# Row maxima and the second norm's later transposes moved from TensorE to VectorE, with a new instruction order

## The chip, the core and the metric

The kernel runs on one core of one Trainium2 chip. The metric is the device time of one execution in microseconds. Fp32 products are made of fp32r pieces: an operand is split into a rounded part and a remainder, and three matmuls (rounded by rounded, and the two cross terms) give the product.

## The reference, cut to what matters

`D` is 512, the sequence 2048 rows in `N` = 4 segments of `L` = 512, with 32 heads of 16.

```python
def _A_ref(x, wq, wk, wv, wo, beta):          # x is the normed input
    # q, k, v: (x @ w) in heads and segments
    mask = (ar[:, None] < ar[None, :]) * (-1e9)
    for s in range(N):
        logits = einsum("bhqd,bhkd->bhqk", qs, ks) * scale + mask
        p = softmax(logits)
        a_dot = einsum("bhqk,bhkd->bhqd", p, vs)
        a_mem = (phi(qs) @ M) / (phi(qs) . z + 1e-6)
        outs.append(g * a_mem + (1.0 - g) * a_dot)
        M = M + phi(ks)^T vs;  z = z + sum phi(ks)
    return o @ wo
def _B_ref(x, w_gate, w_up, w_down):
    return (gelu(x @ w_gate) * (x @ w_up)) @ w_down      # inner width 1376
h  = x + _A_ref(_layernorm(x), ...)
h2 = h + _B_ref(_layernorm(h), ...)
```

## The kernel before, in words

**Attention.** The work is cut into 16 units, one for a chunk of 8 heads and a segment, each in two halves of 4 heads; a half is called `Q` below and there are 32 of them. `qkv` projects a unit (TensorE line L874 for q and k, L913 for v), ScalarE and VectorE split the results, and DMAs lay them out by heads in tiles `stq` and `stk`. `pass_a(Q)` makes all scores of the half once (TensorE L1109), adds the causal mask and takes the negated row maximum on VectorE (L1119, each time followed by a read-out of the accumulator into `nm`). GpSimd splits the maxima in two parts, a rounded one (L1133) and its remainder (L1134), in a 128x32 tile `mm` (the variable `m2`). Two TensorE transposes (L1140), one for 64 partitions each, turn it into two PSUM banks, and two ScalarE copies (L1144) bring both into the 32x128 tile `mx`, of which there is one. A DMA (L1147) writes `mx` into rows of `stq` that were left free for it, so that the next pass's score matmul subtracts the maximum by itself. `pass_b(Q)` makes the scores again, transposed (TensorE L1167), takes the exponential (ScalarE L1173), cuts the diagonal blocks (GpSimd L1181), and multiplies by v (TensorE L1195, in column tiles of 32). Sums, division and the memory part `a_mem` follow through DRAM tiles.

**Feed-forward part.** `wo_seg(s)` multiplies by `wo` and adds x; the sum goes to `h_dram`. `ln2` norms 512 rows and transposes them. The product with the gate and up weights is made for two blocks of 512 rows at once by a scheme with seven products in the place of eight (`ffn`, TensorE L1456), and `down` multiplies by the down weights (TensorE L1520, sum on VectorE L1528). This runs for `p` = 0 and `p` = 1, each 1024 rows. The two calls of `ln2` for `p` = 0 transpose in row tiles of TensorE (`by_side`). The two calls for `p` = 1 load rows again from `h_dram`, norm them on ScalarE (`off`), and transpose them by 16 TensorE matmuls of 128x128 each (L833); of each result ScalarE and VectorE make split blocks.

**Order.** Every helper (`pe`, `act`, `dve`, `pool`, `dma`) only records an operation. `S.run(ORDER)` issues the operations in the sequence of the table `ORDER`, a list of their numbers written out by hand or by a program beforehand; each engine works through its own queue in that sequence. Buffers of a pool are handed out in the same sequence: 35 tiles `row`, 18 tiles `slot`, 8 PSUM banks.

Of the kernel before, what the change touches and what calls it, by code (L numbers as in the profile page):

```python
# [15 lines left out]
P = 128  # L16
# [40 lines left out]
    4, 6, 13, 8, 10, 12, 5, 61, 9, 7, 11, 14, 15, 16, 17, 75, 30, 18, 19, 76, 0, 28, 72, 73, 787, 791, 32, 74,  # L57
    65, 20, 84, 24, 21, 77, 22, 78, 81, 26, 86, 792, 23, 793, 79, 71, 29, 31, 27, 25, 35, 788, 1, 33, 80, 82,
    60, 64, 789, 87, 88, 66, 133, 794, 83, 795, 134, 89, 600, 990, 130, 90, 109, 36, 34, 37, 91, 92, 94, 93, 62,
    85, 2, 98, 38, 135, 99, 39, 994, 995, 996, 796, 110, 797, 104, 103, 43, 131, 111, 798, 112, 67, 799, 42,  # L60
    105, 114, 152, 63, 147, 800, 801, 155, 156, 132, 153, 150, 97, 116, 784, 154, 1386, 96, 142, 143, 113, 144,
    115, 219, 220, 70, 100, 41, 221, 40, 151, 136, 146, 148, 149, 44, 145, 597, 222, 106, 137, 59, 107, 45, 139,
    138, 46, 140, 95, 997, 802, 51, 101, 223, 790, 2085, 49, 141, 157, 52, 47, 158, 102, 224, 803, 53, 56, 48,
    50, 804, 108, 58, 179, 181, 182, 225, 159, 160, 127, 226, 161, 785, 183, 54, 805, 2276, 117, 119, 227, 162,
    57, 163, 118, 180, 404, 129, 228, 55, 165, 229, 164, 205, 174, 176, 178, 230, 405, 233, 806, 208, 177, 209,
    122, 786, 236, 991, 237, 206, 175, 195, 198, 199, 406, 598, 196, 169, 170, 407, 173, 232, 242, 241, 207,
    408, 200, 203, 171, 197, 231, 243, 128, 201, 172, 166, 167, 204, 409, 168, 202, 190, 191, 193, 211, 212,
    234, 184, 807, 410, 214, 411, 808, 185, 186, 244, 235, 3, 194, 192, 187, 1571, 213, 238, 809, 412, 810, 599,
    215, 413, 188, 189, 263, 123, 239, 415, 210, 266, 267, 998, 265, 216, 258, 601, 264, 240, 260, 68, 372, 811,
    262, 414, 261, 259, 416, 812, 289, 217, 246, 245, 124, 591, 373, 292, 293, 294, 290, 291, 1574, 297, 298,  # L70
    295, 296, 252, 374, 813, 814, 815, 253, 999, 254, 279, 375, 255, 376, 1000, 256, 257, 284, 280, 281, 282,
    283, 287, 288, 594, 268, 1001, 218, 1383, 992, 125, 285, 286, 270, 269, 272, 377, 300, 271, 301, 303, 378,
    332, 379, 327, 335, 336, 333, 334, 328, 380, 330, 592, 273, 274, 381, 275, 276, 277, 382, 69, 602, 299, 278,
    393, 304, 331, 394, 302, 305, 386, 383, 329, 384, 385, 400, 763, 306, 319, 764, 320, 321, 390, 348, 395,
    322, 396, 397, 765, 326, 325, 351, 352, 353, 398, 387, 766, 120, 323, 356, 767, 349, 388, 354, 399, 392,
    993, 781, 324, 316, 350, 391, 121, 247, 248, 307, 249, 364, 365, 569, 318, 317, 768, 343, 357, 367, 346,
    443, 344, 447, 769, 358, 445, 770, 359, 403, 126, 361, 444, 438, 446, 355, 366, 442, 441, 347, 771, 337,
    338, 339, 360, 389, 341, 552, 340, 772, 1002, 402, 362, 440, 432, 423, 775, 773, 368, 439, 433, 424, 345,
    363, 593, 434, 369, 342, 448, 774, 370, 474, 1003, 401, 308, 477, 449, 478, 553, 2088, 782, 783, 310, 452,
    417, 554, 475, 371, 419, 450, 418, 459, 476, 555, 451, 435, 462, 469, 460, 463, 311, 472, 556, 461, 436,  # L80
    464, 557, 473, 437, 507, 309, 453, 425, 454, 470, 467, 465, 471, 595, 573, 468, 508, 558, 819, 466, 480,
    483, 747, 559, 510, 481, 512, 560, 576, 574, 511, 312, 313, 509, 513, 455, 479, 516, 250, 1004, 514, 575,
    579, 596, 482, 484, 485, 456, 1190, 561, 577, 562, 578, 251, 457, 458, 563, 502, 1005, 1191, 504, 503, 515,
    564, 1192, 1193, 568, 486, 567, 1006, 565, 506, 499, 581, 523, 505, 1194, 566, 816, 580, 314, 487, 524, 538,
    1007, 1195, 541, 542, 501, 496, 525, 500, 498, 497, 1196, 528, 539, 540, 526, 527, 529, 530, 1197, 531, 532,
    533, 517, 623, 1198, 426, 626, 536, 625, 537, 627, 624, 733, 1008, 534, 535, 488, 315, 544, 734, 751, 1200,
    518, 1199, 1380, 612, 613, 571, 1202, 1201, 614, 519, 547, 735, 520, 628, 490, 817, 521, 522, 489, 631, 630,
    736, 632, 737, 615, 629, 543, 617, 548, 616, 491, 818, 545, 570, 603, 583, 649, 604, 605, 1009, 546, 738,
    650, 652, 639, 640, 642, 641, 739, 654, 618, 619, 622, 621, 657, 658, 620, 653, 655, 549, 550, 644, 647,
    740, 645, 660, 663, 661, 427, 633, 634, 741, 428, 1010, 1011, 656, 648, 572, 584, 635, 742, 743, 492, 636,  # L90
    1012, 637, 429, 430, 431, 1013, 754, 582, 752, 651, 420, 755, 638, 753, 643, 646, 744, 659, 662, 664, 745,
    756, 665, 759, 666, 955, 757, 719, 1014, 585, 720, 758, 421, 1015, 1016, 1017, 1018, 683, 586, 684, 746,
# [1530 lines left out]
```

## Time and profile before

| what | value |
|---|---|
| median of 3 runs | 762.25 us (759.47 to 766.43) |
| profiled execution | 760.04 us |
| its span, first to last instruction | 758.3 us |
| granted TensorE clock | 0.999 |
| instructions | 18030 |
| DMA packets | 70346, 103.66 MB |

The span is what the profile's rows divide up; the profiled execution's own time is 1.7 us longer. Attention fills the span up to about 400 us, the feed-forward part the rest. PE is TensorE's matmul, PEld its weight load, DVE VectorE, ACT ScalarE, POOL GpSimd and SP the engine that issues nearly all DMAs.

### The profile page before, as it was taken

How to read it: one execution, taken by the hardware profiler on the slowest of the kernel's cores; microseconds unless marked ns; L12 is line 12 of the kernel's file. 1: busy time of each engine (PE TensorE's matmuls, PEld its weight loads, DVE VectorE, ACT ScalarE, POOL GpSimd, SP SyncE). 2: the span in 40 equal slices, each digit the busy share in tenths (PEclk: the TensorE clock that was granted, in tenths of full speed). 3: DMA queues.
4: the chain of work that ended last, by engine and by line, in shares of the span. 5: the costliest groups of instructions: out<-in, count | busy, mean ns of one | idle time of the engine just before them, and what ended most of it. 6: DMA issues, size and time to landing. Idle time of an engine off the chain costs nothing.

```text
span 758.3 us, 18030 instructions
## 1 busy us (share of the span) xinstructions
PE 740.1 (98%) x6222; PEld 588.0 (78%) x6222; DVE 579.6 (76%) x1786; ACT 504.5 (67%) x1060; POOL 481.8 (64%) x748
## 2 busy tenths in 40 slices
PE   7899999999999999999999999899999999999997
PEld 5787877768778777776768788788888878888886
DVE  6798789988888898899977455865679645666566
ACT  5887987888776878867685455566675455544640
POOL 6454534644544656677985678786789577869740
PEclk9999999999999999999999999999999999999999
DMA  7666466764666675776658553322123260000002
GB/s 266 174 189 162 119 166 177 193 160 125 173 174 175 174 211 172 197 211 185 193 190 271 185 198 114 119 70 70 56 67 122 70 222 0 1 1 0 1 1 111
DMA packets 70346, 103.66 MB, mean 137 GB/s; under 512 B 12800, under 2 KB 23600, under 8 KB 70256
## 3 DMA queue, kind: packets, MB, share of 16 engines
q1 hardware_dynamic: 69952, 102.13, 46.4%
q8 instruction: 49, 0.80, 0.4%
q10 hardware_dynamic: 304, 0.39, 0.2%
q14 instruction: 41, 0.34, 0.1%
HBM read 54.92 MB, written 21.43 MB: 101 GB/s over the span
## 4 chain that ended last, share of the span: by engine, by line
PE 53%; DVE 3%; POOL 3%; ACT 1%; issue 1%; DMA 0%; POOLq 0%
PE bank L1456 26%; PE bank L1520 15%; PE bank L1275 3%; PE bank L1268 2%; PE bank L1195 2%; PE bank L1167 1%; PE bank L1109 1%; PE bank L874 1%; DVE bank L1119 1%; POOL row L1181 1%; POOL row L1433 1%; POOL slot L1426 1%; PE bank L833 0%; DVE row L1528 0%; DMA r_dram<-z 0%
## 5 line engine op out<-in xcount | busy, mean ns | idle before, releaser
L1173 ACT ACTIVATE row<-bank 128x512 f32<-128x512 f32 x306 | 164.1, 605 | 30.0 <-PE bank L1167 27.6
L1181 POOL TENSOR_SCALAR_AFFINE_SELECT row<-row 128x256 f32<-128x256 f32 (+1 forms) x306 | 106.1, 368 | 104.6 <-ACT row L1173 102.0
L1119 DVE CUSTOM_DVE_ANT_0 aside<-bank,amask 128x128 f32<-128x128 f32 (+2 forms) x384 | 141.2, 419 | 17.0 <-PE bank L1109 9.1
L874 PE MATMUL bank<-slot,slot 64*128 64x512 f32 x720 | 113.7, 404 | 0.7 <-DVE nm L1119 0.6
L1456 PE MATMUL bank<-slot,slot 128*128 128x512 f32 (+1 forms) x381 | 102.3, 391 | 0.0
L1119 DVE CUSTOM_DVE_ANT_0 bank<-bank,amask 128x512 f32<-128x512 f32 x128 | 86.2, 711 | 6.5 <-PE bank L1109 5.7
L1109 PE MATMUL bank<-stk,stq 64*128 64x128 f32 (+3 forms) x512 | 85.5, 333 | 1.9 <-issue 0.7
L1167 PE MATMUL bank<-stq,stk 64*128 64x512 f32 (+3 forms) x512 | 84.4, 337 | 1.2 <-DVE nm L1119 0.7
L1456 PEld LDWEIGHTS bank<-slot,slot 128*128 128x128 f32 (+1 forms) x381 | 70.2, 186 | 16.5 <-DVE bank L1309 0.4
L1528 DVE TENSOR_TENSOR row<-row,bank 128x512 f32<-128x512 f32 x84 | 55.6, 679 | 35.8 <-PE bank L1520 35.6
L874 PEld LDWEIGHTS bank<-slot,slot 64*128 64x128 f32 x720 | 74.9, 185 | 6.7 <-DVE nm L1119 1.2
L1195 PE MATMUL bank<-row,vaug 128*32 128x512 f32 (+3 forms) x982 | 77.2, 435 | 1.0 <-DVE nm L1119 0.2
L1426 POOL TENSOR_TENSOR slot<-row,slot 128x512 fp32r<-128x512 f32 (+3 forms) x52 | 59.5, 1148 | 26.9 <-ACT slot L1424 26.8
L1109 PEld LDWEIGHTS bank<-stk,stq 64*128 64x128 f32 x512 | 59.7, 184 | 14.9 <-DVE nm L1119 4.6
L1167 PEld LDWEIGHTS bank<-stq,stk 64*128 64x128 f32 x512 | 56.9, 185 | 15.2 <-DVE nm L1119 4.0
L1520 PE MATMUL bank<-slot,slot 128*128 128x512 f32 (+2 forms) x231 | 60.4, 387 | 0.0
L1195 PEld LDWEIGHTS bank<-row,vaug 128*32 128x32 f32 x982 | 30.5, 109 | 35.9 <-issue 30.6
L913 PE MATMUL bank<-slot,slot 64*128 64x256 f32 x672 | 54.4, 284 | 0.1
L913 PEld LDWEIGHTS bank<-slot,slot 64*128 64x128 f32 x672 | 49.7, 186 | 1.3 <-DVE slot L971 0.8
L668 POOL TENSOR_TENSOR slot<-row,slot 128x512 fp32r<-128x512 f32 (+1 forms) x33 | 42.7, 1297 | 12.5 <-ACT slot L663 12.3
L1520 PEld LDWEIGHTS bank<-slot,slot 128*128 128x128 f32 (+1 forms) x231 | 43.0, 188 | 9.1
L1119 DVE DVE_READ_ACCUMULATOR2_ANT nm<- 128x1 f32 x512 | 49.8, 97 | 0.1
(263 smaller groups left out, 1650.1 us busy)
## 6 DMA issues: line engine op xcount, KB each, us to landing
stq<-slot SPq DMA_DIRECT2D x96, 128.0 KB
stk<-slot SPq DMA_DIRECT2D x94, 128.0 KB
pv_dram<-row SPq DMA_DIRECT2D x32, 256.0 KB
row<-x SPq DMA_DIRECT2D x29, 256.0 KB
row<-r_dram SPq DMA_DIRECT2D x26, 256.0 KB
row<-h_dram SPq DMA_DIRECT2D x21, 256.0 KB
row<-wg SPq DMA_DIRECT2D x18, 256.0 KB
row<-wd SPq DMA_DIRECT2D x18, 256.0 KB
```

The costliest lines, as they stand in the source:

```text
L874: return nc.tensor.matmul(pm[i].t, w[i].t[rows_of(r), wi, dc * P:(dc + 1) * P], XT[s][dc].t[rows_of(r), xi, :], start=(dc, wi, xi, ph) == ...
L913: return nc.tensor.matmul(pms[n].t[:, 256 * t:256 * t + 256], XT[s][dc].t[rows_of(r), xi, t0:t0 + P], whl[wi].t[rows_of(r), dc // 2, 256 * ...
L1109: nc.tensor.matmul(sa.t[:, c0:c0 + w], sq.t[own, p, i * P:(i + 1) * P], sk.t[own, p, 0:w], start=True, stop=True, tile_position=(64 * a, 0 ...
L1119: nc.vector.tensor_tensor_reduce(out=(sa.t[:, c0:c0 + w] if i > 2 else aside[:, turns[0]:turns[0] + w]), in0=sa.t[:, c0:c0 + w], in1=amask ...
L1167: nc.tensor.matmul(sc.t[:, c0:c0 + D - q0], sk.t[own, p, q0:q0 + P], sq.t[own, p, q0:D], start=True, stop=True, tile_position=(64 * a, 0), ...
L1173: act(w, prio, lambda sc=sc, e=e: nc.scalar.activation(e.t[:, :w], sc.t[:, :w], AF.Exp), [sc, vtab], [e])
L1181: nc.gpsimd.affine_select(v, v, pattern=pat + [[1, P]], compare_op=OP.is_ge, fill=0.0, base=0, channel_multiplier=-1)
L1195: nc.tensor.matmul(pv.t[32 * n:32 * n + 32, kb * P:D], va.t[:, 136 * kb + 17 * j:136 * kb + 17 * j + 32], e.t[:, lo:lo + D - kb * P], star ...
L1426: pool(0.14 + 2.13e-3 * (hi - lo), prio, lambda: nc.gpsimd.tensor_tensor(v.t[:, 1, :hi - lo], r.t[:, lo:hi], v.t[:, 0, :hi - lo].bitcast(F ...
L1456: nc.tensor.matmul(dst.t[:w], v.t[:, wi, c0 + j * w:c0 + (j + 1) * w], b[bk][j].t[:, xi, :], start=first and j == 0 and n == 0, stop=j == ...
L1520: nc.tensor.matmul(pm.t[:, cs], HH[p, f, s].t[:w, hi, t * P:(t + 1) * P], v.t[:w, wi, cs], start=f == fl[0] and n == 0, stop=f == fl[-1] a ...
L1528: dve(W_, prio, lambda a=a, pm=pm, cs=cs, to=to: nc.vector.tensor_tensor(to.t[:, cs], a.t[:, cs], pm.t[:, cs], op=OP.add), [pm, a], [to])
```

## The change

The maxima: the two TensorE transposes and the two ScalarE copies of a half are replaced by four VectorE transposes of 32x32, from `m2` straight into `mx`. The two PSUM banks are no longer taken.

The second norm, for `p` = 1: VectorE transposes each normed 128x512 tile in 32x32 blocks into another `row` tile. Four DMAs for each tile store it, 32 partitions each, to a DRAM tile `t_dram` so that the blocks land in transposed places (runs of 32 elements, 128 bytes). Four DMAs for each norm load 128x512 tiles back, and ScalarE copies each into a PSUM bank, where the split goes on as before.

The table `ORDER` is new as a whole. Lines of the changed kernel that have a counterpart stand 10 to 14 lines further down.

```diff
@@ ORDER
-    4, 6, 13, 8, 10, 12, 5, 61, 9, 7, 11, 14, 15, 16, 17, 75, 30, 18, 19, 76, 0, 28, 72, 73, 787, 791, 32, 74,
+    6, 10, 8, 12, 5, 9, 7, 11, 84, 0, 1, 75, 14, 15, 16, 18, 72, 73, 4, 771, 2, 970, 13, 81, 17, 19, 28, 74,
...
+    t_dram = dram.tile([2, D, D], F32, name="t_dram")
...
@@ layer_norm(..., swap=None)
+        vt = Val()
+        for t in range(4) if swap is not None else []:
+            q = Val(PN)
+            dve(D, prio, lambda t=t, q=q: nc.vector.transpose(q.t, rows[t].t), [rows[t]], [q])
+            for a in range(4):
+                dma(prio, lambda t=t, q=q, a=a: nc.sync.dma_start(bass.AP(
+                    tensor=swap.tensor, offset=swap.offset + t * P + 32 * a,
+                    ap=[[D, 32], [32 * D, 16], [1, 32]]), q.t[32 * a:32 * a + 32]), [q], [vt], kb=480, dur=0.5,
+                    chain=True)
+        for dc in range(ND) if swap is not None else []:
+            dma(prio, lambda dc=dc: nc.sync.dma_start(rows[dc].t, swap[dc * P:(dc + 1) * P]), [vt], [rows[dc]])
         for dc in [] if by_side else range(ND):
             pt = Val(PD)
-
-            def tr(dc=dc, pt=pt):
-                for t in range(4):
-                    nc.tensor.transpose(pt.t[:, t * P:(t + 1) * P],
-                                        rows[t].t[:, dc * P:(dc + 1) * P], ident)
-            pe(4 * TR, prio, tr, [*rows, vident], [pt], acq=acq[dc] if acq else [dst[dc]])
+            if swap is not None:
+                act(D, prio, lambda dc=dc, pt=pt: nc.scalar.activation(pt.t, rows[dc].t, AF.Copy), [rows[dc]], [pt],
+                    acq=acq[dc] if acq else [dst[dc]])
+            else:
+                def tr(dc=dc, pt=pt):
...
@@ pass_a
-        m2, pts, mx = Val(PMM), (Val(PA), Val(PA)), Val(PMX)
+        m2, mx = Val(PMM), Val(PMX)
...
         def turn():
-            for i, pt in enumerate(pts):
-                own = rows_of(i)
-                nc.tensor.transpose(pt.t[0:32, 0:64], m2.t[own].bitcast(F32).rearrange("p a r i -> p (a r i)"),
-                                    ident[own, own], tile_position=(64 * i, 0))
-        pe(rr(64), prio, turn, [m2, vident], pts, acq=[mx], head=0.12, mode="r")
-        for i, pt in enumerate(pts):
-            act(64, prio, lambda i=i, pt=pt: nc.scalar.activation(
-                mx.t[:, 64 * i:64 * i + 64], pt.t[0:32, 0:64], AF.Copy), [pt], [mx], src=0.13, chain=True)
+            for i in range(4):
+                own = slice(32 * i, 32 * i + 32)
+                nc.vector.transpose(mx.t[:, own], m2.t[own].bitcast(F32).rearrange("p a r i -> p (a r i)"))
+        dve(330, prio, turn, [m2], [mx])
...
@@ the second norm of p = 1
-                    ln2(B[1], rows, s, prio, True, PD)
+                    ln2(B[1], rows, s, prio, True, PD, swap=t_dram[s])
```

Where the turn stands. Before, on TensorE, in the sixth half: scores of the next half, the two transposes, then a projection.

```order
L1109 MATMUL bank_70<-stk_92,stq_97 128x512
L1109 MATMUL bank_67<-stk_92,stq_97 128x512
L1140 MATMUL bank_71<-ident,mm_155 32x64
L1140 MATMUL bank_66<-ident,mm_155 32x64
L874 MATMUL bank_72<-slot_75,slot_86 128x512
L874 MATMUL bank_65<-slot_75,slot_85 128x512
```

Now, on VectorE, in the eleventh half, at the place with the fewest instructions between the last maximum of the half (written to `nm_152`) and its turn (which reads `mm_154`, made from it by GpSimd). ISA is the masked maximum and, with 128x1, the read-out that follows it.

```order
L1133 ISA bank_68,nm_152<-bank_68,amask 128x512
L1133 ISA nm_152 128x1
L1133 ISA bank_65,nm_152<-bank_65,amask 128x512
L1133 ISA nm_152 128x1
L545 COPY tock<-bank_68 128x1
L1154 STREAM_TRANSPOSE mx_156<-mm_154 32x32 x4
L1133 ISA aside,nm_153<-bank_65,amask 128x384
L1133 ISA nm_153 128x1
L1133 ISA aside,nm_153<-bank_65,amask 128x128
```

The turn has left TensorE's queue and stands in VectorE's, ahead of maxima of the next half.

The second norm. Before, on TensorE, in the feed-forward part: groups of four transposes between products of `ffn`.

```order
L1456 MATMUL bank_66<-slot_82,stq_100 128x512 x3
L833 MATMUL bank_67<-ident,row_122 128x128
L833 MATMUL bank_67<-ident,row_121 128x128
L833 MATMUL bank_67<-ident,row_128 128x128
L833 MATMUL bank_67<-ident,row_103 128x128
L1456 MATMUL bank_71<-slot_81,slot_86 128x512 x3
```

Now, on SP: the stores of the turned tiles (L833 of the changed kernel) and the first loads (L838) stand between loads of feed-forward weights (`wg`) and of rows of `h_dram`.

```order
L833 DMA t_dram<-row_124 32x16x32 x2
L833 DMA t_dram<-row_107 32x16x32
L833 DMA t_dram<-row_124 32x16x32
L1560 DMA row_126<-h_dram 128x512
L833 DMA t_dram<-row_107 32x16x32 x3
L838 DMA row_112<-t_dram 128x512
L833 DMA t_dram<-row_132 32x16x32
L838 DMA row_127<-t_dram 128x512
L1429 DMA row_102<-wg 128x512
```

On ScalarE the copies into PSUM (L842) stand between splits of weights and steps of the gate (L1434, L1494, L1473).

```order
L1494 ACTIVATE slot_80<-row_132 128x512
L842 ACTIVATE bank_70<-row_112 128x512
L1494 ACTIVATE stk_94<-row_134 128x512
L663 ACTIVATE slot_84<-row_115 128x512
L1434 ACTIVATE slot_74<-vaug_142 128x256
L856 ACTIVATE slot_87<-bank_70 128x512
```

TensorE has no instruction of the second half's norm any more; DMAs on SP's queue and copies on ScalarE's take their place.

More of the change, by code (lines that the diff above doesn't have):

```diff
@@ L686, in split_wv, with layer_norm @@
                 chain=True)
-    def layer_norm(prio, rows, dst, off=False, keep=None, acq=None, done=(), behind=(), scratch=None, by_side=False):
+    def layer_norm(prio, rows, dst, off=False, keep=None, acq=None, done=(), behind=(), scratch=None, by_side=False, swap=None):
         bn, mv = Val(PBN), Val(PMV)
@@ L1298, in blocks, with ln2 @@
         return {k: [Val(PBL), Val(PBL)] for k in ("11", "21", "t1", "22", "t3", "t2", "t4")}
-    def ln2(b, rows, i, prio, off, scratch=None, by_side=False):
+    def ln2(b, rows, i, prio, off, scratch=None, by_side=False, swap=None):
         ys = [Val(PC), Val(PC)] if i else []
@@ L1345, in ln2 @@
         if i == 0:
-            layer_norm(prio, rows, [*b["11"], *b["21"]], off=off, scratch=scratch, by_side=by_side)
+            layer_norm(prio, rows, [*b["11"], *b["21"]], off=off, scratch=scratch, by_side=by_side, swap=swap)
         else:
             layer_norm(prio, rows, [None] * 4, off=off, keep=keep, by_side=by_side,
-                       acq=[[y, t] for y, t in zip(ys, ts)] + [[], []], scratch=scratch)
+                       acq=[[y, t] for y, t in zip(ys, ts)] + [[], []], scratch=scratch, swap=swap)
     ln1(0)
```

4 lines of the change are left out of this document (added), and 507 rows, old and new, of the table ORDER.

## The prediction

> **What bounds the kernel now.** I read the first page, then the busy times by stage, then the rows of the instructions that the change touches. The page first: engines with their share of the span, then the engines of the chain that ended last.
>
> ```profile
> PE 740.1 (98%) x6222; PEld 588.0 (78%) x6222; DVE 579.6 (76%) x1786; ACT 504.5 (67%) x1060; POOL 481.8 (64%) x748
> PE 53%; DVE 3%; POOL 3%; ACT 1%; issue 1%; DMA 0%; POOLq 0%
> ```
>
> TensorE is busy nearly always and its matmuls make up most of the chain. That is an average over two stages, so the busy times by stretch (us; columns PE, PEld, DVE, ACT, POOL, clock, DMA share, GB/s) come next. Attention runs to about 400 us, the feed-forward part from there.
>
> ```profile
> 20.00:400.00 380.00, 373.15 (x4568) 287.99 (x4567) 334.79 (x1367) 300.97 (x669) 221.31 (x488) 1.00 0.64 176
> 340.00:380.00 40.00, 38.51 (x387) 28.85 (x385) 38.47 (x157) 28.43 (x62) 32.21 (x62) 1.00 0.67 188
> 400.00:740.00 340.00, 338.06 (x1502) 276.39 (x1502) 220.03 (x364) 192.20 (x368) 247.82 (x234) 1.00 0.28 87
> 440.00:480.00 40.00, 38.06 (x167) 30.77 (x166) 24.06 (x42) 22.44 (x48) 32.66 (x32) 1.00 0.43 133
> 480.00:520.00 40.00, 40.00 (x178) 33.09 (x178) 24.94 (x60) 28.06 (x57) 28.13 (x29) 1.00 0.29 85
> 520.00:560.00 40.00, 40.00 (x184) 33.12 (x183) 27.51 (x44) 27.64 (x52) 33.70 (x32) 1.00 0.19 53
> ```
>
> The feed-forward stage is TensorE alone: 338.06 of 340 us, with VectorE at 65% (220.03/340) and ScalarE at 57%. There a microsecond off TensorE is a microsecond off the end. Attention is different: TensorE 373.15 of 380, but VectorE 334.79 (88%) and ScalarE 300.97 (79%), and between 340 and 380 us VectorE stands at 38.47 of 40. VectorE has 45.2 us idle in the whole stage; the change spends some of it.
>
> **The change part by part: the turned maxima.** Thirty-two times, two matmuls (L1140) turn a 128x32 tile of maxima and two ScalarE copies (L1144) bring it from PSUM into mx. First the rows of these lines (count, shortest/median/longest ns), then what TensorE waited for ahead of L1140, then TensorE's timeline around one turn.
>
> ```profile
> L1140 PE MATMUL bank<-ident,mm x64: 212/214/230, 33.3 to 382.1; 64*32 64x64 f32 x64
> L1144 ACT ACTIVATE mx<-bank x64: 194/200/240, 33.5 to 382.4; 32x64 f32<-32x64 f32 x64
>   issue: 0.8, 2
>   ACT row L1173: 0.3, 2
>   POOL row L1181: 0.2, 1
>   DVE nm L1119: 0.2, 1
> 42.05 1.50 PE L913 MATMUL bank<-slot,slot 64*128 64x256 f32 x22
> 43.35 0.21 PE L1140 MATMUL bank<-ident,mm 64*32 64x64 f32 x1
> 43.38 0.36 PE L913 MATMUL bank<-slot,slot 64*128 64x256 f32 x2
> 43.51 0.21 PE L1140 MATMUL bank<-ident,mm 64*32 64x64 f32 x1
> 43.54 0.83 PE L913 MATMUL bank<-slot,slot 64*128 64x256 f32 x10
> 44.17 0.33 PE L1109 MATMUL bank<-stk,stq 64*128 64x384 f32 x1
> ```
>
> A matmul's 214 ns is not its price, since neighbours overlap. From start to start, 22 projections take 43.35 - 42.05 = 1.30 us, 59 ns each. From 42.05 to 44.17 there are 34 of them and one turn: 2.12 - 34 x 0.0591 = 0.11 us for the turn. Times 32 that is **3.5 us** off TensorE, plus the waits ahead of L1140, 0.8 + 0.3 + 0.2 + 0.2 = **1.5 us**. ScalarE loses 64 x 0.200 = 12.8 us, of which I book nothing: it has 79 us idle there.
>
> What comes on VectorE: 4 transposes of 32x32 per turn, 128 in all, which no row shows. The nearest rows are VectorE's instructions over very few columns, one read-out of an accumulator and one step of the norm. The second pair are GpSimd's two instructions that make the tile to be turned, and the last five are waits on TensorE, four of its weight loads and one of its matmuls, that the row maxima (L1119) ended.
>
> ```profile
> L1119 DVE DVE_READ_ACCUMULATOR2_ANT nm<- 128x1 f32 x512 | 49.8, 97 | 0.1
> L748 DVE SCALAR_TENSOR_TENSOR bank<-bank,ln 128x4 f32<-128x4 f32 x18 | 3.0, 165 | 0.3
> L1133 POOL CAST mm<-nm 128x16 fp32r<-128x16 f32 x32 | 6.6, 205 | 32.1 <-DVE nm L1119 19.1 <-DVE tock L546 13.0
> L1134 POOL TENSOR_TENSOR mm<-nm,mm 128x16 fp32r<-128x16 f32 x32 | 7.2, 224 | 1.9
> PEld bank L1109 <- DVE nm L1119: 4.6, 16, 0.8
> PEld bank L1167 <- DVE nm L1119: 4.0, 14, 0.5
>   PEld bank L1195: 1.4, 5
>   PEld bank L874: 1.2, 2
>   PE bank L1167: 0.7, 3
> ```
>
> So 128 x 0.097 = 12.4 us if they run back to back like the read-outs, 128 x 0.165 = 21.1 us if each waits out the last like the norm's steps. The four of a turn are independent and only the first waits, so I take 0.097. Each turn also waits in VectorE's queue for GpSimd's 0.205 + 0.224 us. In the new order a median of six VectorE instructions stand between the last maximum of a half and its turn; in five of the 32 turns it is one to five, worth under 0.9 us by their rows. If GpSimd comes late, the maxima of the next half (L1119) queue behind the turn, and TensorE's next scores wait for their banks. I add 1 us for that, so VectorE has 13.4 us more against 45.2 us idle.
>
> What of it reaches TensorE? The listed waits on L1119 are 4.6 + 4.0 + 1.4 + 1.2 + 0.7 = 11.9 us of its load or matmul side; most weight loads run under earlier matmuls, and only the 0.7 us is TensorE's own. If waits grow as the idle time shrinks, by 45.2/(45.2 - 13.4) = 1.42, the loss is between 0.42 x 0.7 = 0.3 and 0.42 x 11.9 = 5.0 us. I take **1.7 us**, below the middle, because the path from maximum to DMA also loses its place in TensorE's queue and two ScalarE copies. Below nothing it could be a gain of up to the 3 us or so that such shorter paths free; above 5 lies the second rival.
>
> **The second norm.** Its two later calls drop 32 TensorE transposes (L833). Their timeline around two of the eight groups of four:
>
> ```profile
> 547.85 0.85 PE L1456 MATMUL bank<-slot,stq 128*128 128x512 f32 x3
> 548.53 0.60 PE L833 MATMUL bank<-ident,row 128*128 128x128 f32 x4
> 548.89 1.64 PE L1456 MATMUL bank<-slot,slot 128*128 128x512 f32 x6
> 550.36 0.86 PE L1456 MATMUL bank<-slot,stq 128*128 128x512 f32 x3
> L833 PE MATMUL bank<-ident,row x28: 270/272/273, 548.5 to 569.8; 128*128 128x128 f32 x28
> ```
>
> Three matmuls take 548.53 - 547.85 = 0.68 us, nine 2.04. From 547.85 to 550.36 there are nine and one group: 2.51 - 2.04 = 0.47 us. Times eight, **3.8 us**, in a stage where TensorE sets the end.
>
> In their place: eight VectorE block transposes of 128x512 (by the 0.68 us of its other 512-column rows, 5.4 us, beside 120 us idle), eight ScalarE copies into PSUM (0.6 us each, 4.8 us, beside 148 us idle), 32 stores of 64 KB in runs of 128 bytes and eight loads. SP spends 0.575 us on issuing one DMA of short runs, so 18 us for the stores; queued behind them are the weight loads of the following tiles and, behind those, ScalarE's splits. The rows for the bytes and for SP:
>
> ```profile
> q1 hardware_dynamic: 69952, 102.13, 46.4%
> DMA packets 70346, 103.66 MB, mean 137 GB/s; under 512 B 12800, under 2 KB 23600, under 8 KB 70256
> L1147 SPq DMA_DIRECT2D stq<-mx x32: 539/575/1047, 33.9 to 384.5; - x32
> SPq L1533 <- DVE row L1528: 144.0, 11, 124.2
> L1528 DVE TENSOR_TENSOR row<-row,bank 128x512 f32<-128x512 f32 x84 | 55.6, 679 | 35.8 <-PE bank L1520 35.6
> L1173 ACT ACTIVATE row<-bank 128x512 f32<-128x512 f32 x306 | 164.1, 605 | 30.0 <-PE bank L1167 27.6
> ```
>
> The stores make 32 x 512 = 16,384 packets. At the mean packet (0.464 x 16 x 758.3 us / 69,952 = 80 ns, of mostly 2 KB) they would hold 16 engines for 82 us; by bytes (2.1 MB at 137 GB/s) for 15 us. Between 440 and 560 us the shares 0.43, 0.29 and 0.19 leave 84 us free. I take the lower end, since a packet of 128 bytes is nearer to its bytes than to a 2 KB packet, and book nothing; the cover is these 84 us. SP's waits of up to 124.2 us for the outputs show that it has room.
>
> [...]
>
> **Order.** The whole order is new. TensorE changes between row-tiled and column-tiled work 81 times before and 79 times now, so nothing is booked.
>
> **Sum.** -3.5 - 1.5 + 1.7 - 3.8 = -7.1 us against the profiled 760.04 us (its span 758.3 plus 1.7 around it): 752.9. That execution lies 2.2 us below the median of the three runs, 762.25; against the median I forecast **755.2 us**, -0.9%. A measurement of this kernel tells about 1% from no change (759.47 to 766.43), so this stands at the edge.
>
> **Rivals.** (1) *TensorE is not the bound of attention.* Its weight loads fill only 287.99 of 380 us there, and VectorE is at 88%; then the 3.5 + 1.5 us of the turns become waits elsewhere and only the second norm's 3.8 us stay: 758.5 us. Against it: so few waits of TensorE's own that L1119 ended. [...] Chance 0.24.
>
> (2) *VectorE becomes the bound of attention: slower.* Place: the maxima between 20 and 400 us, VectorE at 96% from 340 to 380 already. If no order gets VectorE above its present 88%, its 334.79 + 12.4 us need 347.2/0.881 = 394 us, 14 more; less the norm's 3.8 that is 772.6. With 0.165 each, 355.9/0.881 = 404, 24 more: 782. It decides once VectorE needs over some 92% of the shortened stage (347/375 = 92.6%). Against it: the new order puts other maxima between a half's last maximum and its turn nearly everywhere. Chance 0.17.
>
> (3) *The round trip is late.* If packets cost the full 80 ns, or SP's 18 us of issues delay the weight loads, ScalarE stalls on a copy from t_dram, and TensorE behind it. Decided from the point where the stores need more than the 84 us; each further 10 us costs about that: 765 or more. Chance 0.04.
>
> (4) *The new order itself is better*, with fewer waits than counted here: of attention's 380 us only 6.9 are open on TensorE by its busy time, so at most that, less than the same again: 746 to 752. Chance 0.15.
>
> The forecast keeps 0.40, spread over 752 to 758; 0.27 of it and rival 4 make faster by over 1% (below 754.6) likely at 0.42. Within 1%: the forecast's other 0.13 and rival 1: 0.37. Slower by over 1%: rivals 2 and 3: 0.21. Range 746 to 770: rival 4's end, and most of rival 2's lower price; the forecast's own is 752 to 758.
>
> **What would show it.** Right: TensorE rows of L1140 and L833 gone with neighbours at unchanged starts; block transposes near 0.1 us; VectorE near 347 us in attention at about 93%; feed-forward still at 99% TensorE and shorter by 3 to 4 us; attention shorter by 3 to 4 us. Wrong: waits of weight loads on L1119's successor above 20 us, VectorE idle ahead of the turns for GpSimd by over 3 us, transposes above 0.2 us, or TensorE idle between 520 and 600 us with a DMA from t_dram as releaser.

## The result, and the profile after

The changed kernel takes 765.94 us (median, 764.75 to 767.71), the kernel before 762.63 us (759.47 to 766.43): a ratio of 1.004, 95% interval 1.0027 to 1.0053. It is slower by some 3.3 us. The time lies in the predicted range of 746 to 770 us, but on the other side of the kernel before than the forecast of 755.2 us.

The page first: engines with their share of the span, then the engines of the chain that ended last.

```profile
PE 739.2 (97%) x6126; PEld 583.7 (77%) x6126; DVE 610.5 (80%) x1922; ACT 503.3 (66%) x1004; POOL 479.6 (63%) x748
PE 74%; DVE 17%; issue 3%; ACT 3%; DMA 2%; SPq 1%; POOL 0%; DVEq 0%; ACTq 0%; POOLq 0%
```

VectorE had 3% of the chain and now has 17%. The busy times by stretch (columns PE, PEld, DVE, ACT, POOL, clock, DMA share, GB/s) say where:

```profile
20.00:400.00 380.00, 366.43 (x4410) 281.29 (x4409) 355.97 (x1499) 290.51 (x597) 212.46 (x471) 0.99 0.63 175
340.00:380.00 40.00, 38.34 (x427) 27.00 (x426) 38.83 (x158) 31.45 (x63) 29.68 (x59) 1.00 0.67 196
400.00:740.00 340.00, 337.86 (x1552) 273.55 (x1553) 225.29 (x378) 199.75 (x382) 249.14 (x247) 1.00 0.35 102
```

In attention VectorE is busy 355.97 of 380 us, 93.7%, where it was 88.1%. The feed-forward stage is TensorE's alone, as it was. The rows of the new instructions (count, shortest/median/longest ns, first and last start) come from the views of their lines; the second row is the first turn in VectorE's timeline (start, length):

```profile
L1154 DVE STREAM_TRANSPOSE mx<-mm x128: 142/199/206, 37.2 to 390.7; 32x32 f32<-32x32 f32 x128
...
37.20 0.84 DVE L1154 STREAM_TRANSPOSE mx<-mm 32x32 f32<-32x32 f32 x4
...
  POOL mm L1148: 0.9, 3
...
L831 DVE STREAM_TRANSPOSE row<-row x7: 687/703/714, 476.7 to 518.7; 128x512 f32<-128x512 f32 x7
L833 SPq DMA_DIRECT2D t_dram<-row x32: 303/481/695, 478.8 to 544.9; - x32
L842 ACT ACTIVATE bank<-row x7: 580/595/614, 554.8 to 583.5; 128x512 f32<-128x512 f32 x7
```

A 32x32 transpose takes 199 ns. The four of the first turn take 0.84 us together, so some 0.212 us pass from one start to the next, and 128 of them are 27.1 us of VectorE, not 12.4. It waits for GpSimd hardly ever (0.9 us, 3 times). The round trip is done in time: the last store is issued at 544.9 us, the first copy runs at 554.8, and none of these copies waits for a DMA.

The first and the last turn cut the span in three. Before, L1140 ran from 33.3 to 382.1 us of 758.3; now L1154 runs from 37.2 to 390.7 of 762.9. So the start is 3.9 us longer, the middle 4.7 us (348.8 to 353.5), and the rest 4.0 us shorter (376.2 to 372.2), close to the second norm's forecast 3.8. Two things went wrong, one in the middle and one at the start. At the start, TensorE's timeline of before and then of after (start, length, engine, line; in brackets idle time before it and what ended it):

```profile
16.80 5.91 PE L926 MATMUL bank<-slot,slot 128*128 128x256 f32 x48
23.21 0.96 PE L1109 MATMUL bank<-stk,stq 64*128 64x256 f32 x9 [0.50 <-DMA stk<-slot]
```

```profile
17.92 5.91 PE L940 MATMUL bank<-slot,slot 128*128 128x256 f32 x48
28.30 1.33 PE L1123 MATMUL bank<-stk,stq 64*128 64x384 f32 x8 [4.46 <-DMA stq<-slot]
```

The first scores come 5.1 us later, because q and k are split later on VectorE (L985, at 22.68 us against 17.41 before), and they are laid out by DMAs only then. These are single executions: in the runs below that begin in the order of the kernel before and leave the mask where it was, the first scores stand at 23.0 to 25.0 us, and in those that begin in the changed kernel's order at 27.7 to 28.4. VectorE's timeline of after shows what stands ahead of the splits, the building of the head mask (L615 to L620):

```profile
14.61 0.93 DVE L615 CAST row<-row 128x136 int32<-128x136 f32 x1
15.57 1.22 DVE L616 TENSOR_SCALAR row<-row 128x136 int32<-128x136 int32 x1
16.80 3.92 DVE L618 TENSOR_SCALAR row<-row 32x136 f32<-32x136 f32 x3
22.68 1.28 DVE L985 SCALAR_TENSOR_TENSOR slot<-bank,slot 128x512 fp32r<-128x512 f32 x2
```

### The profile page after: what moved, and what is told of

It reads as the page before. It is cut to its first block, busy times and chain, and to the rows that moved or that the text cites. A ratio compares the mean times of both kernels' runs of the same rounds, so it can differ in the third digit from the quotient of the medians.

```text
span 762.9 us, 17952 instructions
## 1 busy us (share of the span) xinstructions
PE 739.2 (97%) x6126; PEld 583.7 (77%) x6126; DVE 610.5 (80%) x1922; ACT 503.3 (66%) x1004; POOL 479.6 (63%) x748
## 4 chain that ended last, share of the span: by engine, by line
PE 74%; DVE 17%; issue 3%; ACT 3%; DMA 2%; SPq 1%; POOL 0%; DVEq 0%; ACTq 0%; POOLq 0%
PE bank L1466 26%; PE bank L1530 14%; PE bank L888 8%; PE bank L1205 7%; PE bank L927 4%; PE bank L1123 4%; PE bank L1177 4%; DVE aside L1133 3%; PE bank L1278 3%; DVE bank L1133 3%; DVE mx L1154 1%; PE bank L1285 1%; PE bank L1091 1%; DVE slot L985 1%; DVE nm L1133 1%
## 5 line engine op out<-in xcount | busy, mean ns | idle before, releaser
L888 PE MATMUL bank<-slot,slot 64*128 64x512 f32 x720 | 117.3, 408 | 0.0
L1466 PE MATMUL bank<-slot,slot 128*128 128x512 f32 (+1 forms) x381 | 103.3, 391 | 1.1 <-DVE row L1538 1.1
L1123 PE MATMUL bank<-stk,stq 64*128 64x256 f32 (+3 forms) x512 | 88.3, 337 | 6.8 <-DMA stq<-slot 4.5
L1466 PEld LDWEIGHTS bank<-slot,slot 128*128 128x128 f32 (+1 forms) x381 | 69.9, 184 | 18.3 <-DVE row L1538 2.0
L1205 PE MATMUL bank<-row,vaug 128*32 128x128 f32 (+3 forms) x976 | 78.1, 437 | 3.6 <-DVE nm L1133 0.9
L1538 DVE TENSOR_TENSOR row<-row,bank 128x512 f32<-128x512 f32 (+1 forms) x91 | 60.1, 676 | 22.6 <-PE bank L1530 22.5
L1436 POOL TENSOR_TENSOR slot<-row,slot 128x512 fp32r<-128x512 f32 (+3 forms) x56 | 63.4, 1141 | 21.9 <-ACT slot L1434 21.9
L1177 PEld LDWEIGHTS bank<-stq,stk 64*128 64x128 f32 x512 | 58.0, 184 | 16.8 <-DVE nm L1133 5.7
L1530 PE MATMUL bank<-slot,slot 128*128 128x512 f32 (+1 forms) x252 | 67.6, 391 | 0.9 <-DVE row L1490 0.6
L1530 PEld LDWEIGHTS bank<-slot,slot 128*128 128x128 f32 (+1 forms) x252 | 47.1, 188 | 12.0 <-DVE row L1490 1.0
```

The costliest lines, as they stand in the source:

```text
L888: return nc.tensor.matmul(pm[i].t, w[i].t[rows_of(r), wi, dc * P:(dc + 1) * P], XT[s][dc].t[rows_of(r), xi, :], start=(dc, wi, xi, ph) == ...
L1123: nc.tensor.matmul(sa.t[:, c0:c0 + w], sq.t[own, p, i * P:(i + 1) * P], sk.t[own, p, 0:w], start=True, stop=True, tile_position=(64 * a, 0 ...
L1177: nc.tensor.matmul(sc.t[:, c0:c0 + D - q0], sk.t[own, p, q0:q0 + P], sq.t[own, p, q0:D], start=True, stop=True, tile_position=(64 * a, 0), ...
L1205: nc.tensor.matmul(pv.t[32 * n:32 * n + 32, kb * P:D], va.t[:, 136 * kb + 17 * j:136 * kb + 17 * j + 32], e.t[:, lo:lo + D - kb * P], star ...
L1436: pool(0.14 + 2.13e-3 * (hi - lo), prio, lambda: nc.gpsimd.tensor_tensor(v.t[:, 1, :hi - lo], r.t[:, lo:hi], v.t[:, 0, :hi - lo].bitcast(F ...
L1466: nc.tensor.matmul(dst.t[:w], v.t[:, wi, c0 + j * w:c0 + (j + 1) * w], b[bk][j].t[:, xi, :], start=first and j == 0 and n == 0, stop=j == ...
```

## The experiments

The theory at first, A: the new order loses some 5 us at the start, the turns cost some 3 us of VectorE, and TensorE's saving is real. The rival B: the turns on VectorE are the whole loss. All ratios are to the kernel before, with 95% intervals. "Middle" is the time from the first turn to the last in the profiled run, and VectorE's share is that of 20 to 400 us.

| run | us | ratio | middle, us | VectorE |
|---|---|---|---|---|
| before | 762.63 | 1 | 348.8 | 88.1% |
| the change | 765.94 | 1.004 [1.0027, 1.0053] | 353.5 | 93.7% |
| turn_only | 778.22 | 1.021 [1.0188, 1.0231] | 365.6 | 90.1% |
| turn_only_one_block | 762.02 | 0.9997 [0.9981, 1.0013] | 347.1 | 88.7% |
| turn_only_off_path | 777.35 | 1.0194 [1.0172, 1.0216] | 362.7 | 90.7% |
| swap_before | 757.75 | 0.9944 [0.9924, 0.9965] | 348.3 | 88.3% |
| both_old_order | 774.78 | 1.0184 [1.016, 1.0207] | 365.3 | 90.0% |
| one_block | 753.5 | 0.9879 [0.9852, 0.9905] | 342.7 | 90.5% |
| off_path | 763.55 | 1.0021 [1.0008, 1.0034] | 352.9 | 93.6% |
| doubled | 797.96 | 1.0468 [1.0448, 1.0488] | 387.6 | 92.0% |
| pe_added | 769.37 | 1.0092 [1.0071, 1.0113] | 353.9 | 93.7% |
| turn_undone | 786.69 | 1.0334 [1.0307, 1.0361] | 372.3 | 84.0% |
| start_mended | 762.9 | 1.0008 [0.9991, 1.0025] | 353.9 | 94.1% |
| start_of_before | 769.81 | 1.0098 [1.0073, 1.0124] | 359.6 | 92.1% |

### One part at a time

The turns alone (turn_only): the kernel before with the change's `turn` and its own order, VectorE's turn in the place of TensorE's.

```diff
-        pe(rr(64), prio, turn, [m2, vident], pts, acq=[mx], head=0.12, mode="r")
-        for i, pt in enumerate(pts):
-            act(64, prio, ...)
+        dve(330, prio, turn, [m2], [mx])
```

> The kernel before with its own order; only the turns move: each of the 32 turns is made by four 32x32 transposes on VectorE at the list place of the TensorE turn, and the two ScalarE copies are gone. Theory A (in the changed kernel the new order loses some 5 us in the first 40 us, the turns on VectorE cost some 3 us in attention, and TensorE's saving of 3.5 us is real): the saving and the give-back cancel, 762.6 us within 1.5, ratio 0.998 to 1.002. Rival B (the whole loss of the changed kernel is the 27 us of new VectorE work): slower, 768 to 771 us. The recorded prediction's own terms for this part (-3.5 -1.5 +1.7) would give 759.3 us.

778.22 us, slower by 16: A fails here, and B's 768 to 771 is passed by far: the slowdown is B's, its size is not. The turns undone (turn_undone), the same diff backwards in the changed kernel:

> The changed kernel and its order, with the turns back on TensorE and the two ScalarE copies behind each (23 of 4773 entries moved by 1 to 13 places, so that two banks are free). Theory A: TensorE's 3.5 us come back and the some 3 us of VectorE's wait go, so 765.9 us within 1.5. Rival B: 758 to 761 us, since the new VectorE work is all that was lost.

Neither theory: 786.69 us, 21 us slower than the change. TensorE now stands in its queue at the turns (L1173) until GpSimd has made the remainder, which no wait ahead of L1140 named before. From the list of waits (total us, times, longest):

```profile
PEld bank L1173 <- POOL mm L1167: 5.9, 9, 1.3
PE bank L1173 <- POOL mm L1167: 3.5, 5, 1.1
```

These rows are too few for 21 us; the turns also take two PSUM banks again, and what else costs was not isolated. So in neither order could the turns change engines without a loss. The round trip, first by putting its work back on TensorE (pe_added):

```diff
+                pe(4 * TR, prio, lambda dc=dc, pt=pt: [nc.tensor.transpose(
+                    pt.t[:, t * P:(t + 1) * P], rows[dc].t[:, t * P:(t + 1) * P], ident) for t in range(4)],
+                   [rows[dc], vident], [pt], ...)
                 act(D, prio, lambda dc=dc, pt=pt: nc.scalar.activation(pt.t, rows[dc].t, AF.Copy), ...)
```

> The changed kernel, with 32 TensorE transposes of 128x128 added where the second norm's copies from the row tiles into the banks stand (their result is overwritten by those copies), so that TensorE has the removed work again and all else stays. If the term of the prediction holds (8 times 0.47 us of TensorE, nothing hidden): 765.9 + 3.8 = 769.7 us. If TensorE has slack in that stage: 765.9 to 766.9 us.

769.37 us, 3.4 us above the change by the medians and 4.0 by the ratios (1.0092 - 1.004 = 0.0052): the term holds. Then the round trip alone in the kernel before (swap_before):

```diff
-                    ln2(B[1], rows, s, prio, True, PD)
+                    ln2(B[1], rows, s, prio, True, PD, swap=t_dram[s])
 ORDER = [
-    (before's entries)
+    (before's first 3300 entries, from there on the changed kernel's)
```

> The round trip alone: turns on TensorE and the order of the kernel before for its first 3300 entries (attention and output projection), from there on the changed kernel's order with its block transposes, stores and loads. If the term of -3.8 us of the prediction holds here too: 762.6 - 3.8 = 758.8 us, within 1. If the feed-forward half of the new order gives 1 us of it back, as its lag of TensorE grew by some 1 us more there: 759.8 us. If the transfers come late behind this attention: 762 us or more.

757.75 us, 0.56% (4.3 us) faster than before. The saving is as forecast, though the changed kernel's order of the feed-forward part comes with it. This is the one complete version here that beats both kernels. Both parts with the old order of attention (both_old_order):

```diff
 ORDER = [
-    (the changed kernel's entries)
+    (before's entries for attention, from there on the changed kernel's)
```

> The changed kernel's code (turns on VectorE, round trip) with the order of the kernel before for attention and output projection (its first 3300 entries, less the 64 ScalarE copies that are gone) and the new order from there on. If the parts add: turns +15.6 us (778.2 against 762.6) and round trip -4.9 us give 773.3 us, within 1.5, and the new order of attention is worth the 7 us from there to 765.9. If the new order is worth nothing in itself (the prediction's term of 0): 766 us.

774.78 us: 1.0184 against 1.021 x 0.9944 = 1.0153 from the parts, whose intervals overlap with it. With the changed kernel's own order it is 1.004, so the new order is worth 1.4%, or 11 us by the ratios (9 by the medians). The prediction had put 0 for it.

### VectorE's time or the turn's way

A new pair of theories: V, VectorE sets the pace of attention, and each of its microseconds costs most of one; O, the new order has the turns in idle time already. One transpose of a turn's four, the others left out, in the new order (one_block) and in the old (turn_only_one_block):

```diff
-            for i in range(4):
+            for i in range(1):
                 nc.vector.transpose(mx.t[:, own], ...)
```

> The changed kernel with one of the four 32x32 transposes of each turn; the other three are left out, so 96 of the row maxima of each half segment are zeros. VectorE has 96 x 0.212 = 20.4 us less. Theory V (in attention a microsecond of VectorE is worth some 0.8 us, as the 27.1 us of turns added 21.6 us of lag in the kernel before's own order): 765.9 - 16 = 750 us. Theory O (the new order has the turns in VectorE's idle time already, and what is left of them is the some 3 us of lag between 40 and 400 us): 762.5 to 764 us.

> The kernel before's order with turns on VectorE (778.2 us), with one of the four transposes of each turn, the rest left out as in the run before this one. Theory V: 778.2 - 16 = 762 us. If not the length of the turn but its place costs the 16 us (VectorE or the waiters of the turn held in a queue at the wrong time): 774 to 778 us.

In the old order 20.4 us less of VectorE give 16.2 us (762.02 against 778.22), as theory V put it to the microsecond. In the new one they give 12.4 us, against theory O's 2 to 3. But these runs also shorten the turn's way by 0.64 us. The next two keep the time and shorten only the way, in the old order and the new:

```diff
+        def aside_turns():
+            for i in range(1, 4):
+                nc.vector.transpose(aside[0:32, own], m2.t[own]...)
+        dve(250, prio, aside_turns, [m2], [])
```

> Turns on VectorE in the kernel before's order, with one transpose on the turn's way as in the run with one block (762.0 us), and the other three made right behind it into a scratch tile that nobody reads: VectorE has all four again, but the transfer of the maxima leaves after the first. If VectorE's time is what costs (theory V): 778 us again, within 2. If the turn's way is what costs (0.64 us later for each of 32 halves, 20 us in all): 762 us, within 2.

> The same in the changed kernel and its order: one transpose on the way (753.5 us with that alone), three behind it into scratch. Theory V: 766 us, within 2. The turn's way: 753.5 us, within 2.

777.35 and 763.55 us. In the old order all but some 1 us of the 16 is VectorE's time, in the new one 10 of 12.4 us are. The rest, 1 and 2.4 us, would be the way's, but the intervals of these runs and of those with the whole turn on the way overlap, so the way's part is not shown. Here is the stretch from 20 to 400 us of turn_only:

```profile
20.00:400.00 380.00, 363.48 (x4325) 279.24 (x4326) 342.48 (x1457) 280.44 (x577) 204.37 (x459) 0.99 0.62 167
```

TensorE got 4325 matmuls done in the time in which before did 4568, 243 fewer, of which the turns are only 64, and VectorE stands at 90%. The load the other way, with every transpose made twice (doubled):

```diff
-            for i in range(4):
+            for i in (0, 1, 2, 3, 0, 1, 2, 3):
```

> The changed kernel with each turn's four transposes made twice, so 128 more of them, 27.1 us of VectorE, in the new order. Theory V (VectorE sets the pace of attention): at 0.61 us per us as below the present load 782 us, up to 793 us if no idle time of VectorE is left to take them. If the four transposes stand in idle time of VectorE: 766 to 770 us.

797.96 us: 27.1 us of VectorE cost 32 us. Now the waits on the maxima, few in the kernel before (4.6 us for the weight loads of the scores), are open in the list of waits:

```profile
PEld bank L1123 <- DVE nm L1133: 21.3, 36, 2.4
PE bank L1123 <- DVE nm L1133: 10.4, 17, 2.1
PE bank L1205 <- DVE nm L1133: 3.5, 5, 1.9
```

So a microsecond of VectorE in attention costs 0.5 us below the change's load (10 us for 20.4), 0.75 in the old order (15.3 for 20.4), and 1.2 above the change's load, where the longer way is in the price.

### Cheaper ways to relieve VectorE

A whole turn in one 128x32 transpose and four small transfers (one_instr), and the same with the start mended, below (one_instr_start):

```diff
-            for i in range(4):
-                nc.vector.transpose(mx.t[:, own], m2.t[own]...)
+            nc.vector.transpose(mx.t, m2.t...)                   # mx is 128x32
...
+            for i in range(4):
+                nc.sync.dma_start(rows[:, :, 32 * i:32 * i + 32], mx.t[32 * i:32 * i + 32])
```

> The changed kernel and its order, with the turn as one 128x32 transpose (its four blocks turned in place, side by side by partitions) and four small transfers in place of one, which put the four blocks where the one transfer put them. Between the rows of 0.199 us (32x32) and 0.703 us (128x512) we take 0.2 us for it, so VectorE has some 20 us less. Theory V: 750 us. Theory O: 762.5 to 764 us. If the three added issues on SyncE or a later landing hold the score rows up: 766 us or more.

> The same one 128x32 transpose and four transfers, in the order whose start is mended (mask building behind the first two splits; 762.9 us with four blocks). If start and turns add up: 3 us under the run before this one, 747 us by theory V and 760 to 761 us by theory O.

779.52 us, 1.0221 [1.0194, 1.0248], and 778.98 us, 1.0223 [1.0192, 1.0254]. The transpose is as cheap as hoped, 0.2 us for all four blocks. The loss is the last rival's, on SyncE's side: 128 issues of 0.529 us in place of 32 of 0.575 are 49 us more in its queue, and the score rows land late; no run separates the issues from the landing. The issues, from the view of their line, and then TensorE's wait, which the list of the changed kernel doesn't have:

```profile
L1159 SPq DMA_DIRECT2D stq<-mx x128: 520/529/652, 36.8 to 406.9; - x128
```

```profile
PE bank L1180 <- DMA stq<-mx: 12.3, 14, 2.7
```

Then the last step of the feature map, moved to ScalarE and GpSimd, in the order with the mended start (phi_moved_start) and in the kernel before (phi_moved_before):

```diff
-        dve(D, prio, lambda: nc.vector.scalar_tensor_tensor(
-            r.t, pm.t, 0.0, e.t, op0=OP.max, op1=OP.add), [pm, e], [r])
+        act(D, prio, lambda: nc.scalar.activation(r.t, pm.t, AF.Relu), [pm], [r])
+        pool(1.24, prio, lambda: nc.gpsimd.tensor_tensor(r.t, r.t, e.t, op=OP.add), [e], [r])
```

> The changed kernel with its start mended (762.9 us), and the last step of the feature map, max(x, 0) + e, taken from VectorE: ScalarE writes the relu, GpSimd adds e. VectorE has 24 x 0.685 = 16.4 us less, ScalarE some 15 us and GpSimd some 30 us more. Theory V (a microsecond of VectorE in attention is worth 0.61 us in this order, by the run with one block a turn): 762.9 - 10 = 753 us. Rival: the longer way of the features, or ScalarE's and GpSimd's queues, hold TensorE up as much: 760 to 764 us.

> The same step moved from VectorE to ScalarE and GpSimd in the kernel before, its order and turns as they are. Theory V (VectorE already limits the kernel before: 6.8 us more of VectorE and 3.5 us less of TensorE left the time where it was, so some 0.4 us per us): 762.6 - 7 = 755.5 us. Rival (TensorE limits the kernel before, as the prediction held): 761.5 to 764 us.

780.02 us, 1.0233 [1.0208, 1.0257], and 779.57 us, 1.0217 [1.0184, 1.0249]. Both rivals are passed: VectorE has less to do (81% in phi_moved_before), and the time grows by 17 us. The waits of phi_moved_before name GpSimd, which stood in its queue for ScalarE's relu at 19 places, and TensorE behind it:

```profile
POOL row L916 <- ACT row L915: 35.7, 19, 4.4
PEld bank L1075 <- POOL row L916: 4.2, 3, 2.0
PE bank L1075 <- POOL row L916: 3.3, 3, 1.5
```

These are too few to account for all 17 us; what else the longer way costs was not isolated. Theory V holds for work that is left out or added in place, not for work that is moved.

### The start

The mask building behind the first two splits, one entry of the new order moved (start_mended):

```diff
-    ..., 777, 3, 131, ..., 781, 91, 99, 85, ...      # 3: the mask; 91, 99: the splits
+    ..., 777, 131, ..., 781, 91, 99, 3, 85, ...
```

> The changed kernel with one entry of its order moved: VectorE's building of the head mask goes from ahead of the first two splits of the projections to right behind them. Theory A: the first scores come at 23.5 to 24.5 us in place of 28.3 and the time falls by 4 to 5 us, to 761 to 762 us. Rival B: the lead of 4 us is lost again in attention, because VectorE's load sets the pace there: 764.5 to 766 us.

First scores at 24.31 us and 762.9 us, 3.0 less than the change: A's step, of somewhat less worth than put. The whole start of the kernel before (start_of_before):

```diff
 ORDER = [
-    (the changed kernel's entries)
+    (before's first 310 entries, from there on the changed kernel's)
```

> The changed kernel (turns on VectorE, round trip) with the first 310 entries of the order of the kernel before, some 45 us, and its own from there on (4 of 4741 entries moved by 1 to 3 places). Theory: the whole 5.6 us of the start are the order's, of which moving the mask building gave 3.0: 760 to 761 us. Rival: what is left of the start comes from the turns and VectorE's load, not from the order: 762.5 to 763.5 us, as with the mask building moved.

769.81 us, the wrong way. The first turn does come 3.6 us earlier (33.6), but the middle is 6.1 us longer than the change's (359.6 against 353.5). The mask building, 2.9 us of VectorE, is back in the middle there, and the join disturbs the queues; which of the two it is stays open. Last, the mask building moved to the start in the version with the round trip alone (swap_before_mask):

```diff
 ORDER = [
-    (entry 267: the mask)
+    (the mask, right behind the second split)
```

> The round trip alone (757.75 us) with one entry moved: the building of the head mask, 2.9 us of VectorE at 43 us, in the middle of attention, goes to the start, right behind the first two splits, where VectorE waits. Theory V at 0.44 to 0.8 us per us of VectorE: 1.3 to 2.3 us less, 755.5 to 756.5 us. If VectorE doesn't set the pace there, or the mask's steps wait for GpSimd as in the changed kernel and hold the first evictions up: 757 to 760 us.

761.89 us, 0.9995 [0.9976, 1.0013]: the 4 us won are gone. The mask's steps push the norm's steps behind them in VectorE's queue from 18.4 us (swap_before) to 24.4, ScalarE waits for these, VectorE's queue then stands for ScalarE, and the first maxima start at 27.62 us against 23.68, with the next scores behind them. Not all of this is the mask's: in this one execution the projections ahead of the scores already end at 24.5 us (22.7 in the kernel before), the mean granted clock is 0.993 (1.000 in swap_before's execution), and the first scores were 2.1 us late before that (25.08 against 23.02).

```profile
25.08 0.96 PE L1142 MATMUL bank<-stk,stq 64*128 64x256 f32 x9 [0.56 <-DMA stk<-slot]
28.45 0.79 PE L1142 MATMUL bank<-stk,stq 64*128 64x384 f32 x3 [2.40 <-DVE nm L1152]
```

## Why the prediction was wrong, step by step

**The second norm's saving** was right. Its 3.8 us measured 3.4 to 4.0 (pe_added), and 4.3 with the order that came along (swap_before), and the round trip is hidden, as booked: in the feed-forward part no wait of TensorE on a load from `t_dram` is listed, and the third rival is out. By the shares of queue q1 on the two pages (46.4% of 758.3 us for 69,952 packets, 49.0% of 762.9 us for 88,000, each of 16 engines), the 18,048 packets that came on took by estimate some 19 ns each, not 80. The turns' 3.5 us and the 1.5 us of waits can't be seen by themselves, since no run takes the turns off TensorE and puts them nowhere. turn_only_one_block fits them (6.8 us of VectorE at 0.75 are 5.1 us, and the time stayed), but that price was not measured for the first block.

**The price of a transpose** is the first term that failed. The prediction took 0.097 us each, like the accumulator's read-outs, and 0.165 as the upper bound. It measured 0.199 us, and 0.21 from start to start: 27.1 us of VectorE where 13.4 were booked, one of these for GpSimd. The step that went wrong is "the four of a turn are independent and only the first waits": four 32x32 transposes in a row don't overlap at all. The kernel before had nearer rows than a read-out that moves one column, with 16 and 64 columns:

```profile
64.22 0.28 DVE L1034 TENSOR_TENSOR mb<-bank,mmask 128x64 f32<-128x64 f32 x1 [0.19 <-PE bank L1023]
64.36 0.17 DVE L1037 TENSOR_TENSOR mb<-bank,mmask 128x16 f32<-128x16 f32 x1
64.44 0.26 DVE L1034 TENSOR_TENSOR mb<-bank,mmask 128x64 f32<-128x64 f32 x1
64.57 0.16 DVE L1037 TENSOR_TENSOR mb<-bank,mmask 128x16 f32<-128x16 f32 x1
```

By their lengths, 32 columns take near 0.2 us. But these do overlap, with 0.08 to 0.14 us from start to start, so that the transposes would not was in no row.

**What of it reaches TensorE** failed for a second reason, and would have without the first: at 0.5 to 0.75 us per microsecond the 12.4 us booked would have cost 6 to 9 us, not 1.7. The prediction scaled the listed waits on the maxima, 0.7 to 11.9 us, against 45.2 us of VectorE's idle time. The measured price puts 27.1 us at some 13 us in the new order and 20 in the old. The idle time was not to be had: in turn_only VectorE still idles 37.5 of 380 us, 23.2 of them in waits for TensorE's banks, where it was 22.8 before. A reading that fits is that it waits for scores that TensorE can't make until VectorE has emptied the banks; no run gave TensorE more banks to show it. And the waits are a poor scale. Summed over the lists between 20 and 400 us, TensorE's own on the maxima are 2.2 us before and 2.1 in the changed kernel (10.0 in turn_only), those of its weight loads 14.9 and 15.5 (23.6 in turn_only); the five rows of the prediction were 11.9 of the 17.1 us before. The largest rows, of the changed kernel and then of turn_only:

```profile
PEld bank L1123 <- DVE nm L1133: 7.7, 24, 0.7
...
PEld bank L1120 <- DVE nm L1130: 11.4, 25, 1.1
PE bank L1120 <- DVE nm L1130: 3.9, 10, 0.7
```

So the signs of being wrong that the prediction set on waits (20 us of weight loads on the maxima, 3 us on GpSimd) did not show, though it was wrong; the signs of being right on VectorE (0.1 us a transpose, 347 us in attention) and on a shorter attention failed.

**Order = 0** failed too, and this hid the first two. Without the new order the change would stand at 774.78 us, inside the second rival's 772.6 to 782. That rival had the right mechanism, with its point of decision at 92% (93.7% measured), and a chance of 0.17. That its price fits is partly luck: by its own rule the 27.1 us would have given 361.9/0.881 = 411 us of attention and some 789 us. The new order brings VectorE from 90% to 94% in attention; it is worth 9 to 11 us in all, though it loses some 4 us at the start. The fourth rival, a better order, is there as well, on top of the second, and with more than the 6.9 us it allowed.

It was not the larger share on the page of before that set the price of the turns: of TensorE's 98% and VectorE's 76% it was the 76%, which is 88% in attention.

## What to carry to other kernels

Ask what an engine's share is in the stage that the change touches. In this kernel an engine at 88 to 90% that feeds a loop with another engine already passed half or more of any added work on to the time of the whole, whatever idle time it showed; so price each added instruction by its start-to-start time on that engine, and take at least half of that time as loss until shown otherwise. Price small instructions by their columns: a 32x32 transpose took 0.20 us and a 128x32 one 0.21, so four of the small ones cost four times as much for the same data. And an order made for one place of the work is part of the kernel: here it was worth 9 to 11 us, and moving work between engines in an order made for the other place cost 16 to 21 us each time it was tried.

## What the runs showed of the hardware that was not expected

**TensorE's clock after a pause.** In the changed kernel the 4.46 us of waiting for the first scores are followed by matmuls at a granted clock of 0.50 (third column from the end), until 33 us:

```profile
26.00:27.00 1.00, 0.00 (x0) 0.00 (x0) 0.34 (x2) 1.00 (x4) 1.00 (x4) 0.64 0.99 207
27.00:28.00 1.00, 0.00 (x0) 0.00 (x0) 0.00 (x0) 1.00 (x6) 0.72 (x1) 0.50 0.98 268
28.00:29.00 1.00, 0.70 (x6) 0.73 (x8) 0.00 (x0) 1.00 (x4) 0.00 (x0) 0.50 0.83 285
32.00:33.00 1.00, 1.00 (x8) 0.81 (x6) 0.81 (x6) 0.66 (x2) 0.00 (x0) 0.50 0.90 227
33.00:34.00 1.00, 1.00 (x12) 0.85 (x10) 0.82 (x3) 0.98 (x2) 0.00 (x0) 0.94 0.21 74
```

From 28.3 to 33 us that is 4.7 us of work at a clock of 0.50, so by estimate about 2.3 us lost on top of the pause itself. By these averages the clock fell at some 26.3 us (0.64 over the whole microsecond), 2.4 us into the pause, and was up again at some 33.1 us. In swap_before_mask it is 0.50 from 28 to 34 us, around the end of a pause of 2.40 us (to 28.45 us), and in start_mended 0.50 from 28 to 31 us, behind three pauses of 1.62, 1.28 and 0.66 us. In the kernel before, whose pauses between 8 and 34 us are 1.28 us at most, it is 1.00 throughout. No run here varies the pause alone, so which length brings the clock down is not shown.

**VectorE beside GpSimd.** A 32x136 step of the mask took 3.44 us at 16.8 us in the changed kernel, and 0.22 and 0.23 us right after it. Three steps in a row end within 0.1 us of the end of a GpSimd instruction (the lengths of L618, then the timeline of GpSimd, against L615, L616 and L618 above, which end at 15.54, 16.79 and, the first of three, 20.24):

```profile
L618 DVE TENSOR_SCALAR row<-row x3: 222/228/3442, 16.8 to 20.5; 32x136 f32<-32x136 f32 x3
14.14 1.30 POOL L684 TENSOR_TENSOR slot<-row,slot 128x512 fp32r<-128x512 f32 x1
15.40 1.30 POOL L668 TENSOR_TENSOR slot<-row,slot 128x512 fp32r<-128x512 f32 x1
20.05 0.11 POOL L646 MEMSET vaug<- 128x16 f32 x1
```

That VectorE waited there for GpSimd is a reading that fits; no run here takes GpSimd's work away to show it, and not every GpSimd instruction comes with a longer step of VectorE. In the kernel before, the same steps stand at 43 us: L615 and L616 take 0.22 and 0.23 us beside three instructions of GpSimd's L1181, and only the second L618 takes 1.24 us, to within 0.1 us of the end of a GpSimd L684.

```profile
43.21 0.22 DVE L615 CAST row<-row 128x136 int32<-128x136 f32 x1
43.47 0.23 DVE L616 TENSOR_SCALAR row<-row 128x136 int32<-128x136 int32 x1
43.05 0.91 POOL L1181 TENSOR_SCALAR_AFFINE_SELECT row<-row 128x128 f32<-128x128 f32 x3 [0.18 <-ACT row L1173]
43.93 1.28 POOL L684 TENSOR_TENSOR slot<-row,slot 128x512 fp32r<-128x512 f32 x1
```

The transposes show nothing of the kind: 142 to 206 ns in all 128.
